# A recorded order that lets the vector engine and GpSimd take turns in their shared SBUF ports, with the decode's additions on the vector engine and row maxima kept in PSUM

## Chip, cores and metric

One core of one Trainium2 chip. The metric is the device time of one execution in microseconds (us). Three executions of the kernel before took 1466.68, 1468.1 and 1468.34 us; the median is 1468.1.

## What is computed

Attention over 4 batches, 12 heads, 448 rows and head size 64, with an RMS norm of q and k; its output, 1792 tokens of 768 values, goes through a feed-forward layer with squared ReLU (d_ff 2048) and then a gated one (d_ff 1536). All in float32.

```python
q_n, k_n = (rmsnorm(q, g_q), rmsnorm(k, g_k))
scores = scale * np.matmul(q_n, k_n.transpose(0, 1, 3, 2))
attn = np.exp(scores - np.max(scores, axis=-1, keepdims=True))
attn = attn / (np.sum(attn, axis=-1, keepdims=True) + 1e-09)
x = np.matmul(attn, v).transpose(0, 2, 1, 3).reshape(B * S, H * D)
r = np.maximum(x @ w_in, 0.0)
x = (r * r) @ w_out
g = x @ w_gate
out = (g * (1.0 / (1.0 + np.exp(-g))) * (x @ w_val)) @ w_out2
```

## The kernel before

A float32 operand is split into a high part (float32r, made by a copy that rounds) and a low part (what is left). A product of the feed-forward layers is then three matmuls of a 128x128 weight block with 448 columns: hi*hi, hi*lo and lo*hi (`mm3`, issued in line 301). Every split needs a subtraction, from SBUF to SBUF.

The weights come as float64 words. `load_weights` decodes them in chunks of 128 rows and 384 columns, two chunks for a tile of 128 d_ff values. A chunk is a transfer to a raw buffer, a scaling (line 252, ScalarE), four vector instructions (lines 262, 265, 268 and 271), an addition (275), a rounding copy (193, ScalarE) and a subtraction (288). The additions and subtractions in 275 and 288 are called the decode's additions below. The key of a weight is `in`, `out` (first layer), `g`, `v`, `o2` (second).

The work has two parts. In the first, attention runs pair of heads by pair of heads: scores of a tile of 128 rows (715, 721), their row maxima (742, vector engine), the maxima times 1/rms (745), the exponentials (751, ScalarE), transposes of the probabilities (811 to 820), their split (851), the products with the values (876 to 886). In its gaps stands the "filler": the first six d_ff tiles of the first layer for batches 0 to 2 (`h_a`, `ya`), and three tiles of batch 3 (`h_lead`, `lead`). Twelve weight tiles are decoded in this part.

The second part sweeps over d_ff tiles, batch after batch: `h` tiles (or `h_g` and `h_v`) accumulate in two PSUM banks, and the vector engine reads them out (338, 354, 364) before the bank can be used again; `y` tiles accumulate over the sweep. 112 chunks are decoded here, each when an older weight's room comes free. That gives three bursts of decoding.

No order is written by hand. A model of the engines in the kernel's Python, run while the kernel is built, decides it: a thread yields an instruction with the engines that may run it and how long that takes, and a free engine takes the ready instruction of the lowest rank. The engine named first is the one the instruction is meant for; another takes it only if the first would be done later than the other by a margin (`spare`: 600 ns for ScalarE, 1500 for the vector engine, 500 for GpSimd). Each engine then executes its instructions in that order.

```python
yield {"G": 956, "V": 469}, lambda e: e.tensor_tensor(out=t, in0=t, in1=a, op=ALU.add)
...
job = min(q, key=lambda job: (job[0].rank, job[2]))
done = free_at[e] = clock[0] + p[0][e]
```

The model before knows nothing that two engines share.

Of the kernel before, what the change touches and what calls it, by code (L numbers as in the profile page):

```python
# [9 lines left out]
F32 = mybir.dt.float32  # L10
# [56 lines left out]
WC = 384  # L67
# [3 lines left out]
def attention_two_ffn_kernel(  # L71
# [51 lines left out]
    engines = {"P": nc.tensor, "A": nc.scalar, "G": nc.gpsimd, "V": nc.vector, "S": nc.sync}  # L123
# [19 lines left out]
    def resume(t, value):  # L143
        while True:
# [11 lines left out]
            elif isinstance(p, tuple):  # L156
                job = [t, p, serial[0], False]
                for e in p[0]:
                    queues[e].append(job)
            else:  # L160
                heapq.heappush(timers, (clock[0] + p, serial[0], t, None))
            return

    def late(job):
        """How long the engine that an instruction is meant for would take to be done with it."""
        costs = job[1][0]
        e = next(iter(costs))
        ahead = [o for o in queues[e] if not o[3] and (o[0].rank, o[2]) < (job[0].rank, job[2]) and next(iter(o[1][0])) == e]
        return max(free_at[e] - clock[0], 0) + sum(o[1][0][e] for o in ahead) + costs[e]

    def dispatch(e):
# [3 lines left out]
        q = [job for job in queues[e] if e == next(iter(job[1][0])) or late(job) > job[1][0][e] + spare[e]]  # L175
# [6 lines left out]
        done = free_at[e] = clock[0] + p[0][e]  # L182
# [18 lines left out]
    def simulate(done):  # L201
        """Issues instructions until done()."""
        while not done():
# [13 lines left out]
            times += [free_at[e] for e in engines if queues[e] and free_at[e] > clock[0]]  # L217
            clock[0] = min(times)
# [1113 lines left out]
```

## Time and profile before

| what | value |
|---|---|
| median of three executions | 1468.1 us |
| span of the profiled execution, first to last instruction | 1462.0 us |
| what the median has around that span | 6.1 us |
| TensorE busy / weight loads | 93% / 79% |
| vector engine / ScalarE / GpSimd busy | 61% / 42% / 45% |
| mean granted TensorE clock | 0.971 |
| last row maximum of the attention starts at | 470.9 us |

The profiled execution's time as a whole is not listed apart from its span; the 6.1 us is the difference to the median. The shares are means over parts with different limits, so the profile is read by stretches. A busy time of the vector engine holds whatever an instruction waits inside itself, after it has started.

### The profile page before, as it was taken

Reading aid. Unit: us, or ns where it says so; the run is one execution under the profiler, and the core shown is the slowest. Engines: PE = TensorE matmul, PEld = TensorE weight load, DVE = VectorE, ACT = ScalarE, POOL = GpSimd, SP = SyncE. Lnnn points to the kernel's source line nnn. Section 1 sums busy time; section 2 is a strip of 40 time slices with the busy share of each in tenths; the row PEclk is TensorE's granted clock in tenths of the full one; section 3 lists DMA queues with packets and bytes.
Section 4 is the critical chain, followed back from the end, with each engine's and each line's share of the span. In section 5 each row is a group of like instructions: output and inputs, shape, how many; then the busy total and the mean of one; then the engine's idle time right before and its main releaser. Section 6 shows DMA issues by size and latency. Waiting matters only on the chain.

```text
span 1462.0 us, 18924 instructions
## 1 busy us (share of the span) xinstructions
PE 1358.5 (93%) x6513; PEld 1148.5 (79%) x6513; DVE 897.2 (61%) x1607; ACT 618.2 (42%) x1376; POOL 656.8 (45%) x580
## 2 busy tenths in 40 slices
PE   8888899999999998889999977899999879999999
PEld 5444667776777887769999866799999768999998
DVE  8999999988887199981011999811117992112121
ACT  5766778777877234333121344312113331111110
POOL 4656674554454177763122666622125762021200
PEclk9999999999999999889999998999999999999999
DMA  6666555534531244343030544502113430122121
GB/s 212 207 188 208 144 164 172 163 117 135 165 116 57 68 119 125 115 123 107 7 108 7 154 127 146 179 16 76 37 39 113 134 110 1 44 71 82 32 76 38
DMA packets 79378, 157.22 MB, mean 108 GB/s; under 512 B 11241, under 2 KB 55090, under 8 KB 79282
## 3 DMA queue, kind: packets, MB, share of 16 engines
q1 hardware_dynamic: 79282, 156.02, 34.9%
q8 instruction: 51, 0.84, 0.2%
q14 instruction: 45, 0.37, 0.1%
HBM read 131.04 MB, written 24.94 MB: 107 GB/s over the span
## 4 chain that ended last, share of the span: by engine, by line
PE 48%; DVE 20%; issue 6%; DMA 1%; POOL 1%; ACT 0%; DVEq 0%; ACTq 0%; POOLq 0%; SPq 0%
PE y L301 15%; PE h_g L301 9%; PE h_v L301 9%; PE h L301 5%; PE ya L301 2%; PE sc L721 1%; PE pt L820 1%; DVE wt_v L262 1%; PE h_a L301 1%; DVE wt_o L265 1%; DVE wt_v L265 1%; DVE wt_out L265 1%; DVE wt_g L262 1%; DVE wt_g L265 1%; DVE wt_o L262 1%
## 5 line engine op out<-in xcount | busy, mean ns | idle before, releaser
L301 PE MATMUL h<-x,hi_in 128*128 128x448 f32 x516 | 159.6, 393 | 31.1 <-DVE r L338 27.8
L301 PE MATMUL h_g<-x,hi_g 128*128 128x448 f32 x576 | 168.8, 375 | 21.1 <-DVE sig L354 19.8
L354 DVE TENSOR_TENSOR sig<-h_g,sig 128x448 f32<-128x448 f32 x48 | 29.9, 622 | 257.0 <-ACT sig L353 257.0
L367 POOL TENSOR_TENSOR s<-sig,s 128x448 fp32r<-128x448 f32 x48 | 57.5, 1198 | 260.4 <-ACT s L193 260.2
L301 PE MATMUL h_v<-x,hi_v 128*128 128x448 f32 x576 | 165.2, 368 | 9.8 <-DVE r L338 6.2
L301 PE MATMUL y<-s,hi_o 128*128 128x448 f32 x576 | 163.6, 365 | 0.0
L301 PE MATMUL y<-s,hi_out 128*128 128x448 f32 x552 | 157.7, 367 | 0.0
L751 ACT ACTIVATE ring<-sc,m,rms 128x448 f32<-128x448 f32 x168 | 121.7, 725 | 64.9 <-DVE m L745 51.4
L301 PEld LDWEIGHTS h<-x,hi_in 128*128 128x128 f32 x516 | 103.6, 203 | 45.8 <-DVE r L338 31.9
L301 PEld LDWEIGHTS h_g<-x,hi_g 128*128 128x128 f32 x576 | 110.4, 193 | 33.8 <-DVE sig L354 23.2
L301 PEld LDWEIGHTS h_v<-x,hi_v 128*128 128x128 f32 x576 | 108.6, 189 | 20.0 <-DVE r L338 6.6
L721 PE MATMUL sc<-kst,qst 128*128 128x448 f32 x368 | 115.3, 407 | 8.7 <-ACT ring L751 8.6
L742 DVE TENSOR_REDUCE m<-sc 128x1 f32<-128x448 f32 x168 | 103.1, 615 | 20.1 <-PE sc L721 17.5
L301 PEld LDWEIGHTS y<-s,hi_o 128*128 128x128 f32 x576 | 108.2, 188 | 8.7
L301 PEld LDWEIGHTS y<-s,hi_out 128*128 128x128 f32 x552 | 104.4, 189 | 8.7
L353 ACT ACTIVATE sig<-h_g 128x448 f32<-128x448 f32 x48 | 26.1, 543 | 195.0 <-PE h_g L301 194.9
L301 PE MATMUL h_g<-x,lo_g 128*128 128x448 f32 x288 | 107.1, 372 | 0.0
L301 PE MATMUL h_v<-x,lo_v 128*128 128x448 f32 x288 | 105.6, 367 | 0.0
L301 PE MATMUL y<-s,lo_o 128*128 128x448 f32 x288 | 105.2, 365 | 0.0
L342 POOL TENSOR_TENSOR s<-r,s 128x448 fp32r<-128x448 f32 x40 | 48.8, 1222 | 122.1 <-DVE r L338 111.5
L301 PE MATMUL h<-x,lo_in 128*128 128x448 f32 x258 | 100.6, 390 | 2.7 <-POOL lo_in L288 2.7
L301 PE MATMUL y<-s,lo_out 128*128 128x448 f32 x276 | 101.1, 366 | 0.0
(177 smaller groups left out, 3134.6 us busy)
## 6 DMA issues: line engine op xcount, KB each, us to landing
kq<-in_kq_t_dram SPq DMA_DIRECT2D x46, 448.0 KB
raw_in<-in_w_in_dram SPq DMA_DIRECT2D x32, 384.0 KB
raw_out<-in_w_out_dram SPq DMA_DIRECT2D x32, 384.0 KB
rkb<-rkd SPq DMA_DIRECT2D x46, 224.0 KB
xr<-x2d SPq DMA_DIRECT2D x42, 224.0 KB
raw_g<-in_w_gate_dram SPq DMA_DIRECT2D x24, 384.0 KB
raw_v<-in_w_val_dram SPq DMA_DIRECT2D x24, 384.0 KB
raw_o<-in_w_out_dram SPq DMA_DIRECT2D x24, 384.0 KB
```

The costliest lines, as they stand in the source:

```text
L262: yield {"V": 269}, lambda e: e.tensor_scalar(out=ti, in0=ai, scalar1=3, scalar2=None, op0=ALU.logical_shift_left)
L265: yield {"V": 469}, lambda e: e.scalar_tensor_tensor(out=ti, in0=ai, scalar=SIGN_BIT, in1=ti, op0=ALU.bitwise_and, op1=ALU.bitwise_or)
L301: return {"P": 187}, lambda e: e.matmul(ps, lhsT=w, rhs=x, start=first, stop=last), 0
L342: yield {"G": 1091, "V": 535}, lambda e: e.tensor_tensor(out=s[:, 1, :], in0=r, in1=as_f32(s[:, 0, :]), op=ALU.subtract)
L353: yield {"A": 424}, lambda e: e.activation(out=t, in_=pg, func=ACTF.Sigmoid)
L354: yield {"V": 535}, lambda e: e.tensor_tensor(out=t, in0=pg, in1=t, op=ALU.mult)
L367: yield {"G": 1091, "V": 535}, lambda e: e.tensor_tensor(out=s[:, 1, :], in0=t, in1=as_f32(s[:, 0, :]), op=ALU.subtract)
L721: e.matmul(sc, lhsT=qs[h][:, c, rows], rhs=ks[h], start=(p + c == 0), stop=(p + 1 == len(parts) and c == 1),)
L742: yield {"V": 531}, lambda e: e.tensor_reduce(out=m[:, 0:1], in_=sc, axis=AX.X, op=ALU.max, negate=True)
L751: yield {"A": 704}, lambda e: e.activation(out=probs(n, 0, S), in_=sc, func=ACTF.Exp, bias=m[:, 1:2], scale=rq, accum_out=sums[g][0][:, i: ...
L820: e.transpose(ps[:, bass.ts(t, 128)], probs((first if j < 3 else second) + t, k, 128), ident)
```

## The change

The model gets a port: while a "ported" instruction runs on GpSimd or the vector engine, neither starts another ported one. Everything on GpSimd is ported; on the vector engine, what is issued under the new letter `W` instead of `V`.

```diff
@@ resume @@
-                    queues[e].append(job)
+                    queues["V" if e == "W" else e].append(job)
@@ new, ahead of late @@
+    port = [0.0]
+    def meant(job):
+        e = next(iter(job[1][0]))
+        return "V" if e == "W" else e
+    def cost(job, e):
+        costs = job[1][0]
+        return costs["W"] if e == "V" and "W" in costs else costs[e]
+    def ported(job, e):
+        return e == "G" or e == "V" and "W" in job[1][0]
@@ dispatch (late in the same way) @@
-        q = [job for job in queues[e] if e == next(iter(job[1][0])) or late(job) > job[1][0][e] + spare[e]]
+        q = [job for job in queues[e] if e == meant(job) or late(job) > cost(job, e) + spare[e]]
+        if port[0] > clock[0]:
+            q = [job for job in q if not ported(job, e)]
...
-        done = free_at[e] = clock[0] + p[0][e]
+        done = free_at[e] = clock[0] + cost(job, e)
+        if ported(job, e):
+            port[0] = done
@@ decode, line 275 (288 in the same way) @@
-            yield {"G": 956, "V": 469}, lambda e: e.tensor_tensor(out=t, in0=t, in1=a, op=ALU.add)
+            yield {"W": 469, "G": 956}, lambda e: e.tensor_tensor(out=t, in0=t, in1=a, op=ALU.add)
@@ mm @@
-        return {"P": 187}, lambda e: e.matmul(ps, lhsT=w, rhs=x, start=first, stop=last), 0
+        return {"P": 203}, lambda e: e.matmul(ps, lhsT=w, rhs=x, start=first, stop=last), 0
@@ all_scores @@
-            sc = tile_at(where, [128, S], F32, f"sc{n}")
+            bank = tile_at(where, [128, 512], F32, f"sc{n}")
+            sc = bank[:, :S]
...
-            spawn(softmax(n, sc, where), n, True)
+            spawn(softmax(n, sc, bank[:, S:S + 1], where), n, True)
@@ softmax @@
-        m = tile_at(m_at, [128, 2], F32, f"m{n}")
-        yield {"V": 531}, lambda e: e.tensor_reduce(out=m[:, 0:1], in_=sc, axis=AX.X, op=ALU.max, negate=True)
+        m = tile_at(m_at, [128, 1], F32, f"m{n}")
+        yield {"V": 531}, lambda e: e.tensor_reduce(out=top, in_=sc, axis=AX.X, op=ALU.max, negate=True)
...
-        yield {"V": 69}, lambda e: e.tensor_tensor(out=m[:, 1:2], in0=m[:, 0:1], in1=rq, op=ALU.mult)
+        yield {"V": 130}, lambda e: e.tensor_tensor(out=m, in0=top, in1=rq, op=ALU.mult)
```

All other SBUF-to-SBUF instructions of the vector engine (decode, scaling of k, splits of k, q, v and x, the rsqrt) go from `V` to `W` with their engines in the order they had. More of the model's durations change: score products 374 to 406 a head (748 to 760 for whole ones), transposes 374 to 480, subtractions on GpSimd 1091 to 1106, rsqrt steps 120 to 97. The vector engine is asked before GpSimd. What is computed stays the same.

How this moves instructions, at three places. Names: `wt_`, `wa_` are a chunk's temporaries, `hi_`, `lo_` the parts of the weight, followed by the key and the d_ff tile (`o22_0` is chunk 0 of tile 2 of `o2`).

The vector engine in the second burst, from the read-out of d_ff tile 11 of the last first-layer sweep on, before:

```order
L338 SCALAR_TENSOR_TENSOR r_1_3_11_8839<-h_1_3_11_8796,r_1_3_11_8839 128x448
L262 TENSOR_SCALAR wt_o22_0_8866<-wa_o22_0_8859 128x384
L265 SCALAR_TENSOR_TENSOR wt_o22_0_8866<-wa_o22_0_8859,wt_o22_0_8866 128x384
L288 TENSOR_TENSOR lo_v2_8846<-wt_v2_1_8816,hi_v2_8845 128x384
L268 TENSOR_SCALAR wa_o22_0_8859<-wt_o22_0_8866 128x384
L262 TENSOR_SCALAR wt_o22_1_8887<-wa_o22_1_8880 128x384
L271 SCALAR_TENSOR_TENSOR wa_o22_0_8859<-raw_o22_0_8817,wa_o22_0_8859 128x384
L265 SCALAR_TENSOR_TENSOR wt_o22_1_8887<-wa_o22_1_8880,wt_o22_1_8887 128x384
```

and the same place in the changed kernel:

```order
L356 SCALAR_TENSOR_TENSOR r_1_3_11_8831<-h_1_3_11_8797,r_1_3_11_8831 128x448
L283 SCALAR_TENSOR_TENSOR wt_v2_0_8839<-wa_v2_0_8828,wt_v2_0_8839 128x384
L306 TENSOR_TENSOR lo_g2_8846<-wt_g2_0_8781,hi_g2_8845 128x384
L286 TENSOR_SCALAR wa_v2_0_8828<-wt_v2_0_8839 128x384
L293 TENSOR_TENSOR wt_g2_1_8790<-wt_g2_1_8790,wa_g2_1_8784 128x384
L289 SCALAR_TENSOR_TENSOR wa_v2_0_8828<-raw_v2_0_8802,wa_v2_0_8828 128x384
L280 TENSOR_SCALAR wt_v2_1_8876<-wa_v2_1_8868 128x384
L293 TENSOR_TENSOR wt_v2_0_8839<-wt_v2_0_8839,wa_v2_0_8828 128x384
L306 TENSOR_TENSOR lo_g2_8846<-wt_g2_1_8790,hi_g2_8845 128x384
```

Lines 293 and 306 (275 and 288 before), which stood almost all on GpSimd, now stand between the decode's other steps.

GpSimd at the start of the first burst, before:

```order
L275 TENSOR_TENSOR wt_in7_1_6356<-wt_in7_1_6356,wa_in7_1_6345 128x384
L342 TENSOR_TENSOR s_1_0_3_6371<-r_1_0_3_6372,s_1_0_3_6371 128x448
L288 TENSOR_TENSOR lo_in7_6363<-wt_in7_1_6356,hi_in7_6362 128x384
L275 TENSOR_TENSOR wt_out7_0_6385<-wt_out7_0_6385,wa_out7_0_6374 128x384
L275 TENSOR_TENSOR wt_out7_1_6403<-wt_out7_1_6403,wa_out7_1_6397 128x384
L288 TENSOR_TENSOR lo_out7_6450<-wt_out7_0_6385,hi_out7_6449 128x384
```

and now:

```order
L1164 TENSOR_TENSOR x_1_0_0_6375<-xr_1_0_0_6344,x_1_0_0_6375 128x448
L360 TENSOR_TENSOR s_1_0_3_6387<-r_1_0_3_6388,s_1_0_3_6387 128x448
L1164 TENSOR_TENSOR x_1_0_4_6601<-xr_1_0_4_6583,x_1_0_4_6601 128x448
L1164 TENSOR_TENSOR x_1_0_5_6774<-xr_1_0_5_6745,x_1_0_5_6774 128x448
L360 TENSOR_TENSOR s_1_0_7_6779<-r_1_0_7_6784,s_1_0_7_6779 128x448
```

What stays on GpSimd are splits of activations.

TensorE behind the last scores of the attention, before:

```order
L721 MATMUL sc167_5920<-kst47_5738,qst1_248 128x448 x2
L301 MATMUL ya2_0_5905<-sa2_0_5244,hi_out0_1400 128x448 x2
L301 MATMUL ya2_0_5905<-sa2_0_5244,lo_out0_1401 128x448
L301 MATMUL ya2_0_5905<-sa2_1_5385,hi_out1_1519 128x448 x2
L301 MATMUL ya2_0_5905<-sa2_1_5385,lo_out1_1520 128x448
```

and now:

```order
L740 MATMUL sc167_5807<-kst47_5639,qst1_248 128x448 x2
L319 MATMUL h_a2_0_5680<-x1_16_4691,hi_in0_514 128x448
L319 MATMUL h_a2_0_5680<-x1_16_4691,lo_in0_515 128x448
L319 MATMUL h_a2_0_5680<-x1_17_4899,hi_in0_514 128x448
L838 MATMUL pt163_5826<-ident_205,ring_245 128x64
```

The filler of batch 2 is at its first `h_a` tile there, not at its first `ya` tile: 95 of its matmuls moved behind the last scores.

## Rows read from the trace of the kernel before

**Rows 1.** By stretch: us; PE, PEld, DVE, ACT, POOL busy (instructions); clock; DMA.
```profile
20.00:220.00 200.00, 172.72 (x743) 108.87 (x743) 197.56 (x412) 144.08 (x356) 128.68 (x111) 0.95 0.60 181
220.00:470.00 250.00, 245.15 (x1276) 186.66 (x1275) 219.20 (x464) 196.97 (x478) 125.19 (x110) 0.99 0.44 135
470.00:510.50 40.50, 40.50 (x205) 35.25 (x206) 10.16 (x20) 14.25 (x31) 9.17 (x9) 1.00 0.19 62
510.50:657.00 146.50, 124.00 (x527) 107.76 (x526) 138.97 (x193) 57.65 (x116) 104.17 (x87) 0.90 0.41 120
657.00:800.00 143.00, 143.00 (x707) 132.54 (x707) 16.82 (x28) 32.24 (x62) 35.20 (x31) 1.00 0.18 59
800.00:950.00 150.00, 124.03 (x571) 111.03 (x570) 143.84 (x205) 58.30 (x114) 99.75 (x85) 0.94 0.49 147
...
1100.00:1215.00 115.00, 98.65 (x458) 88.17 (x457) 101.93 (x144) 43.53 (x87) 74.05 (x64) 0.96 0.38 114
```
**Rows 2.** The longest waits between engines: us in total, times, longest.
```profile
ACT ring L751 <- DVE m L745: 51.4, 64, 2.2
...
PE h L301 <- DVE r L338: 27.8, 11, 4.1
...
ACT wa_v L252 <- DMA raw_v<-in_w_val_dram: 21.2, 15, 2.7
```
**Rows 3.** A stretch of the first burst in order of time: start, us, engine, line, instruction.
```profile
568.41 1.31 POOL L288 TENSOR_TENSOR lo_out<-wt_out,hi_out 128x384 fp32r<-128x384 f32 x1
...
568.90 1.24 DVE L275 TENSOR_TENSOR wt_in<-wt_in,wa_in 128x384 f32<-128x384 f32 x1
...
570.06 0.61 DVE L338 SCALAR_TENSOR_TENSOR r<-h,r 128x448 f32<-128x448 f32 x1
...
570.59 0.62 DVE L262 TENSOR_SCALAR wt_out<-wa_out 128x384 int32<-128x384 int32 x1
...
570.72 0.68 PE L301 MATMUL h<-x,hi_in 128*128 128x448 f32 x2 [1.60 <-DVE r L338]
```
**Rows 4.** Views of the tiles wt_out, r and m: shortest/median/longest ns.
```profile
L265 DVE SCALAR_TENSOR_TENSOR wt_out<-wa_out,wt_out x32: 541/547/1404, 99.3 to 640.6; 128x384 int32<-128x384 int32 x32
...
L275 POOL TENSOR_TENSOR wt_out<-wt_out,wa_out x26: 997/1064/2409, 104.8 to 644.3; 128x384 f32<-128x384 f32 x26
...
L338 DVE SCALAR_TENSOR_TENSOR r<-h,r x43: 603/617/626, 527.7 to 894.7; 128x448 f32<-128x448 f32 x43
...
L745 DVE TENSOR_TENSOR m<-m,rms x168: 137/159/1152, 16.5 to 472.0; 128x1 f32<-128x1 f32 x168
```
**Rows 5.** Groups by line: busy us, mean ns of one, idle before.
```profile
L742 DVE TENSOR_REDUCE m<-sc 128x1 f32<-128x448 f32 x168 | 103.1, 615 | 20.1 <-PE sc L721 17.5 <-PE sc L715 1.5
L745 DVE TENSOR_TENSOR m<-m,rms 128x1 f32<-128x1 f32 x168 | 71.9, 429 | 0.7
L457 DVE TENSOR_REDUCE ss<-nat 128x7 f32<-128x448 f32 x48 | 28.9, 607 | 5.5 <-ACT nat L451 5.5
```
**Rows 6.** The attention in order of time, ScalarE, vector engine and GpSimd.
```profile
101.80 1.27 POOL L646 TENSOR_TENSOR qst<-kq,qst 128x448 fp32r<-128x448 f32 x1
101.97 1.12 DVE L745 TENSOR_TENSOR m<-m,rms 128x1 f32<-128x1 f32 x1
...
103.12 0.72 ACT L751 ACTIVATE ring<-sc,m,rms 128x448 f32<-128x448 f32 x1 [0.60 <-DVE m L745]
...
106.24 0.14 DVE L745 TENSOR_TENSOR m<-m,rms 128x1 f32<-128x1 f32 x1
106.31 0.60 DVE L457 TENSOR_REDUCE ss<-nat 128x7 f32<-128x448 f32 x1
```
**Rows 7.** The first burst in order of time, vector engine.
```profile
562.37 0.35 DVE L262 TENSOR_SCALAR wt_in<-wa_in 128x384 int32<-128x384 int32 x1
...
562.64 0.55 DVE L265 SCALAR_TENSOR_TENSOR wt_out<-wa_out,wt_out 128x384 int32<-128x384 int32 x1
...
563.11 0.55 DVE L265 SCALAR_TENSOR_TENSOR wt_in<-wa_in,wt_in 128x384 int32<-128x384 int32 x1
```

More of the change, by code (lines that the diff above doesn't have):

```diff
@@ L116, in attention_two_ffn_kernel @@
     ctx.enter_context(tc.manual_schedule())
-    engines = {"P": nc.tensor, "A": nc.scalar, "G": nc.gpsimd, "V": nc.vector, "S": nc.sync}
+    engines = {"P": nc.tensor, "A": nc.scalar, "V": nc.vector, "G": nc.gpsimd, "S": nc.sync}
     settle = {"P": 195, "A": 160, "V": 125, "G": 150, "S": 0}
@@ L162, in resume @@
             return
+    port = [0.0]
[7 more added lines that the diff above has]
+        return e == "G" or e == "V" and "W" in job[1][0]
     def late(job):
[L166 to L169, printed above, removed]
+        e = meant(job)
+        ahead = [o for o in queues[e] if not o[3] and (o[0].rank, o[2]) < (job[0].rank, job[2]) and meant(o) == e]
+        return max(free_at[e] - clock[0], 0) + sum(cost(o, e) for o in ahead) + cost(job, e)
     def dispatch(e):
@@ L217, in simulate @@
             times += [free_at[e] for e in engines if queues[e] and free_at[e] > clock[0]]
+            times += [port[0]] * (port[0] > clock[0])
             clock[0] = min(times)
@@ L628, in prep_k @@
         if e == "A":
-            yield {"V": 535, "G": 1091}, lambda e: e.tensor_tensor(out=kr, in0=kr, in1=rk, op=ALU.mult)
+            yield {"W": 535, "G": 1106}, lambda e: e.tensor_tensor(out=kr, in0=kr, in1=rk, op=ALU.mult)
         rk_free.append(rk_at)
@@ L724, in products @@
                         )
-            yield {"P": 748 if full else 374 * len(parts)}, products, 0
+            yield {"P": 760 if full else 406 * len(parts)}, products, 0
             scored[0] = n + 1
@@ L732, in all_scores, with softmax @@
                 kq_free.append(kq_at.pop(g))
-            spawn(softmax(n, sc, where), n, True)
-    def softmax(n, sc, where):
+            spawn(softmax(n, sc, bank[:, S:S + 1], where), n, True)
+    def softmax(n, sc, top, where):
         g, i = divmod(n, PT)
@@ L751, in softmax @@
         yield {"A": 704}, lambda e: e.activation(
-            out=probs(n, 0, S), in_=sc, func=ACTF.Exp, bias=m[:, 1:2], scale=rq, accum_out=sums[g][0][:, i:i + 1]
+            out=probs(n, 0, S), in_=sc, func=ACTF.Exp, bias=m, scale=rq, accum_out=sums[g][0][:, i:i + 1]
         )
@@ L770, in norms @@
         z, at = sums[g]
-        yield {"V": 73}, lambda e: e.tensor_scalar(out=z, in0=z, scalar1=EPS_SUM, scalar2=None, op0=ALU.add)
+        yield {"W": 73}, lambda e: e.tensor_scalar(out=z, in0=z, scalar1=EPS_SUM, scalar2=None, op0=ALU.add)
         yield {"V": 119}, lambda e: e.reciprocal(z, z)
@@ L888, in products @@
                         )
-            yield {"P": 748 if full else 374 * (1 + (j == 3))}, products, 0
+            yield {"P": 760 if full else 406 * (1 + (j == 3))}, products, 0
             pt_free.extend(at)
@@ L940, in outputs @@
         zb, zb_at = zinv.pop(g)
-        yield {"G": 1091, "V": 535}, lambda e: e.tensor_tensor(out=ox, in0=ox, in1=zb, op=ALU.mult)
+        yield {"G": 1106, "W": 535}, lambda e: e.tensor_tensor(out=ox, in0=ox, in1=zb, op=ALU.mult)
         zb_free.append(zb_at)
```

58 lines of the change are left out of this document (29 added, 29 removed).

## Prediction

> **What bounds the kernel now.** I read the busy times by stretch first. Between 657 and 800 us TensorE starts 707 matmuls in 143 us, one per 0.2023 us, at a granted clock of 1.00 [rows 1]: that is its pace when nothing holds it. Three other stretches fall short, and they are the three bursts of decoding: 527 matmuls in 146.5 us (724 at that pace, so 197 or 39.9 us lost), 571 in 150 us (741 would fit, 34.5 us lost), 458 in 115 us (568, 22.3 us lost), with the clock down at 0.90 to 0.96 [rows 1]. In them the vector engine is busy 95%, 96% and 89% of the time, while in the free stretch it is busy 12% [rows 1]. Of the 951 us after the attention, 97 are lost here.
>
> Next the waits: the longest one of TensorE that is worth anything is for the read-out of an `h` bank, 27.8 us in 11 waits [rows 2]. The stretch at 568 us shows why the read-out is late. GpSimd runs a subtraction from 568.41 for 1.31 us; the vector engine starts an addition at 568.90 that ends at 570.14, 0.42 us after GpSimd's end; the read-out `r` follows at 570.06 and the next `h` at 570.72, with TensorE idle for 1.60 us [rows 3]. The tile views say that this is the rule: a decode step on SBUF takes 541 ns at its shortest and 1404 at its longest, a read-out from PSUM 603 to 626 [rows 4]. So the two engines exclude each other for whole instructions where the vector engine works from SBUF to SBUF, and not where it reads PSUM. A busy vector engine here is partly a waiting one.
>
> In the attention the same exclusion hits the softmax. The product of a row maximum with 1/rms is one column; it takes 137 ns at its shortest [rows 4] and 429 on the mean of 168 [rows 5]. At 101.97 us it lasts 1.12 us, beside a GpSimd instruction that runs from 101.80 to 103.07, and ScalarE's exponential starts 0.03 us after its end [rows 6]. ScalarE waits 51.4 us in total for this step [rows 2].
>
> **The change, part by part.** Durations that count on a full engine are spacings from start to start: 0.53 us for 448 columns (570.06 to 570.59 [rows 3]), 0.47 and 0.27 for 384 columns with two inputs or one [rows 7], 0.07 for the product of the maxima [rows 6]. For the other small steps I take 0.10, between that and its shortest duration of 0.14. The sum is against the span, 1462.0 us; the median is 6.1 us above it, and I add these at the end.
>
> *Attention.* From the order I count the vector engine's instructions up to the attention's last output rows. Before: 458 of 448 columns, 58 and 59 of 384 (two inputs, one), 203 small, 168 products: 242.7 + 27.3 + 15.9 + 20.3 + 11.8 = 318 us. Now: 446, 100, 52, 203, 168, the product at 0.14: 236.4 + 47 + 14 + 20.3 + 23.5 = 341 us. The 42 additional decode steps cost 20 us; 22 of 43 scalings of k go to ScalarE, which has room (72% and 79% busy [rows 1]). About 10 us of either sum lie behind the last scores (20 instructions [rows 1]). So of the 470 us up to them, 308 were work and 162 were waits of all kinds, 49 of these in the products of the maxima alone (168 x (429 - 137) ns).
>
> Those 49 us go, because the product now has one input in PSUM, and such instructions were not held [rows 4]. Its price from PSUM is not shown; a reduction of 448 columns takes 615 ns from PSUM and 607 from SBUF [rows 5], 8 ns apart. I take 0.14, its shortest whole duration instead of its spacing. The Trainium skill (Perfetto Trace Analysis, Optimizing Scalar/DVE Operations) gives about 60 ns of access per vector instruction on SBUF and 125 on PSUM. By that rule the product would cost 65 ns more, an estimate of 11 us for 168, where the row's 8 ns make 1.3 us; the 12 us that I have put in cover either.
>
> Of the remaining 113 us of waits I take off 20: GpSimd's instructions up to there fall from 239 to 206, the order is made with the exclusion known, and less filler presses on TensorE. That leaves 93, and the last scores at 332 + 93 = 425 us, where they were at 470. Against that, 95 matmuls of filler moved behind the last scores: 95 x 0.2023 = 19 us more in the stretch that took 40.5 [rows 1]. The attention with its tail ends at 485 instead of 510.5: **-26 us**. Bounds: 60 us of waits give -59; 126 give +7.
>
> *First burst.* GpSimd has 85 instructions from the first to the last split of this sweep, and now 13; the vector engine goes from 192 instructions (75 us at the spacings) to 266 (110 us). If GpSimd's 13 at 1.15 us each (between the median of 1.06 [rows 4] and the 1.31 and 1.27 of the timelines [rows 3, 6]) hold it every time, that makes 15 us more, 125 in all. The last decode step stands just ahead of the read-out of tile 13, and 4 x 18 matmuls remain behind it, 14.6 us, less 2 that overlap: 137.5 against 146.5, **-9 us**. TensorE needs 105.6 for its 522 matmuls and the vector engine 110, so 118 is the lower end. At the upper end the order hurts: 48 decode steps and three splits stand between the read-outs of tiles 3 and 4, 21 us in which TensorE runs dry. I put 155 there.
>
> *Second burst.* TensorE has nine tiles of 36 and six of 54 matmuls, 131 us. The vector engine has 116 us (84 before), GpSimd 23 instructions (90 before), 26 us, of which 34 instructions on PSUM can hide 18. So 124 to 142 us; I take 141, a loss of 10 instead of 34.5: **-24.5 us**, between -34.5 and -12.
>
> *Third burst.* 486 matmuls, 98 us; vector engine 82 us (58 before) and 13 GpSimd instructions (61 before), 15 us. A loss of 6 instead of 22.3: **-16 us**, between -22 and -6.
>
> The other edits (matmuls taken as 203 instead of 187, transposes as 480, shorter rsqrt steps) alter only where the model places things; their effect is in the orders I counted.
>
> Sum: -26 - 9 - 24.5 - 16 = -75.5, a span of 1386.5 and a time of **1392.6 us**. With all ends at once, 1331 to 1472.
>
> **The rivals.**
>
> *The waits only change hands (no gain in the attention).* GpSimd still runs 206 instructions there, some 237 us at 1.15. What the product no longer waits for, the next SBUF step waits for: 119 us of waits leave the end of the attention's tail where it is. Bursts: 0, -17 and -11. Time 1468 - 28 = 1440. For it: a GpSimd as busy as this is met by every second instruction. Against: the steps that then wait are not the ones ScalarE waits for.
>
> *Slower: the waits all stay in the attention.* If all 162 us remain, the last scores come at 494 and the tail ends 43 us late; first burst +9, second -12, third -6. Time 1468 + 34 = 1502. With the bursts like that, it decides from 128 us of waits on. Against it stand the 49 us that belong to one kind of instruction.
>
> *The additions cost in full.* A vector engine busy 139 of 146.5 us [rows 1] has no room, if that time is work: 74 more steps in the first burst, 60 in the second and 48 in the third are 35 + 28 + 22.5 us at 0.47, and 20 + 19 in the attention with its tail. Time 1468 + 125 = 1593. The Trainium skill (Perfetto Trace Analysis, Optimizing Scalar/DVE Operations) says that with a saturated vector engine, giving work to ScalarE or even GpSimd may make sense; by that rule this change goes the wrong way. The trace speaks against it: that busy time holds waits, 75 us being work by the count above. In the same place the Trainium skill adds that the two share a read port, so that moving work between them might not help.
>
> *Hidden anyway: the raw transfers set the bursts' pace.* ScalarE's first decode step waits for a transfer, 21.2 us for `v` alone [rows 2]. If that is the limit, nothing is gained in the bursts nor, with 119 us of waits, in the attention: 1468. Against it: those waits are on ScalarE, which is 39% busy there [rows 1], while the vector engine hardly stands idle.
>
> **How the numbers follow.** Forecast 0.70, waits that change hands 0.17, transfers 0.05, slower 0.06, additions in full 0.02. The range 1350 to 1445 holds most of the forecast's own bounds and the first rival; the rest, some 2 in 10, lies outside. Within 0.2% is about what a measurement of this kernel can tell from no change: faster 0.70 + 0.17 + 0.02, the same 0.03 (the transfers' middle), slower 0.06 + 0.02.
>
> **What would show it.** In the profile of the changed kernel: the product of the maxima at a mean below 200 ns; decode steps near their shortest durations; GpSimd's busy time down by about 225 instructions; 640 matmuls or more in 141 us of the second burst, where 571 took 150; the last row maximum at about 425 us and the end of the filler at about 485. It is wrong if ScalarE still waits some 50 us for the product, if the last maximum stays at 470, or if TensorE still loses 30 us or more in the second burst.

## The result, and the profile after

The changed kernel takes 1419.96 us in the median of four executions (1409.75 to 1429.86), the kernel before 1467.39 beside it: a ratio of 0.9683, 95% interval 0.963 to 0.9736. It is faster, by less than the 75 us that were forecast. The profiled execution took 1429.86 us, the longest of the four; its span is 1427.7, 34.3 us under the 1462.0 of before.

The busy times by stretch of the changed kernel; the stretches are the attention's two halves, its tail (from the last row maximum to the end of the filler), the first burst, the free stretch, and the second and third burst:

```profile
core 0: us, PE busy (x) PEld busy (x) DVE busy (x) ACT busy (x) POOL busy (x), PEclk, DMA share, GB/s
20.00:220.00 200.00, 173.47 (x747) 110.03 (x746) 180.25 (x434) 154.61 (x377) 87.22 (x73) 0.93 0.56 174
220.00:461.90 241.90, 235.25 (x1214) 175.41 (x1212) 199.48 (x482) 199.78 (x485) 125.88 (x110) 0.98 0.47 148
461.90:520.00 58.10, 58.10 (x293) 52.04 (x294) 11.75 (x22) 19.71 (x41) 15.63 (x14) 1.00 0.13 43
520.00:665.00 145.00, 116.73 (x524) 104.17 (x523) 118.97 (x267) 60.04 (x118) 28.59 (x15) 0.89 0.40 121
665.00:800.00 135.00, 135.00 (x655) 122.61 (x654) 14.53 (x24) 28.49 (x54) 34.06 (x30) 1.00 0.20 62
800.00:950.00 150.00, 150.00 (x727) 136.22 (x727) 133.59 (x279) 65.42 (x127) 44.74 (x25) 1.00 0.48 152
1100.00:1215.00 115.00, 115.00 (x558) 104.44 (x557) 83.55 (x173) 41.77 (x82) 31.37 (x15) 1.00 0.33 103
```

Against [rows 1] the second burst starts 727 matmuls in 150 us where it started 571, the third 558 in 115 us where it started 458: TensorE stands still in neither. The first burst still gives 524 in 145 us. The attention did not end earlier: the tail is 58.1 us long, the last row maximum came at 462.0 us (470.9 before), the filler ended at 520.1 (510.7 before). And the free stretch is slower at the same granted clock of 1.00: 135 us for 655 matmuls is 0.2061 us each, where [rows 1] gave 0.2023.

Two lines of the grouping by shape, for the product of the maxima and the exponentials:

```profile
L765 DVE TENSOR_TENSOR m<-sc,rms 128x1 f32<-128x1 f32 x168 | 25.0, 150 | 1.4
L771 ACT ACTIVATE ring<-sc,m,rms 128x448 f32<-128x448 f32 x168 | 121.5, 724 | 32.9 <-DVE m L765 21.7 <-PE pt L834 10.3
```

and the busy times of the page with, under them, four lines of its 40 slices of 35.7 us each:

```profile
PE 1358.5 (95%) x6511; PEld 1142.0 (80%) x6511; DVE 814.3 (57%) x1822; ACT 635.8 (45%) x1408; POOL 437.1 (31%) x355
...
PE   8898798999999995969999999999999999999998
...
DVE  6898899888877249990010399951116992112121
...
POOL 2443454564653320131313142322122240121200
PEclk8999899999999998989999999999999999999999
```

The product has fallen from 429 to 150 ns [rows 5], ScalarE's waits for it from 51.4 to 21.7 us [rows 2]. GpSimd has 355 instructions, 225 fewer than before. In the slices the vector engine's bursts are still there (9 9 9 from the sixteenth on, then two more), but TensorE has a digit under 9 only in the attention, in the first of them and in the last slice, and the clock only in the first two. Of the signs that the prediction listed, those for the mechanism are there; those for the end of the attention (a last row maximum at about 425 us, the end of the filler at about 485) are not.

From the starts of the matmuls in both traces: end of the filler +9.4 us, the 522 matmuls of the first burst -0.9 (145.6 to 144.7), the breaks of the second and third burst -34.6 and -22.3 (to zero), and +15.3 from the slower pace of the 3831 matmuls after the last break (206.7 ns from start to start, 202.7 before). Together -33.1 of the -34.3. Of the +9.4, 3.0 are there before the tenth row maximum (40.4 us after the start, 37.4 before).

### The profile page after: what moved, and what is told of

Its sections match the earlier page's. It is cut to its first block, busy times and chain, and to the rows that moved or that the text cites. A ratio compares the mean times of both kernels' runs of the same rounds, so it can differ in the third digit from the quotient of the medians.

```text
span 1427.7 us, 18828 instructions
## 1 busy us (share of the span) xinstructions
PE 1358.5 (95%) x6511; PEld 1142.0 (80%) x6511; DVE 814.3 (57%) x1822; ACT 635.8 (45%) x1408; POOL 437.1 (31%) x355
## 4 chain that ended last, share of the span: by engine, by line
PE 79%; DVE 10%; DMA 5%; ACT 3%; issue 2%; POOL 1%; SPq 0%; DVEq 0%; ACTq 0%; POOLq 0%
PE y L319 22%; PE h_g L319 13%; PE h_v L319 13%; PE h L319 9%; PE ya L319 4%; PE sc L740 4%; PE pt L840 4%; PE h_a L319 3%; PE o L901 2%; PE o L906 2%; PE pt L838 1%; DVE wa_out L289 1%; DMA nat<-in_q_n_dram 1%; DVE sc L762 1%; ACT ring L771 1%
## 5 line engine op out<-in xcount | busy, mean ns | idle before, releaser
L319 PE MATMUL h<-x,hi_in 128*128 128x448 f32 x516 | 153.3, 379 | 23.2 <-DVE r L356 23.1
L385 POOL TENSOR_TENSOR s<-sig,s 128x448 fp32r<-128x448 f32 x47 | 73.3, 1560 | 327.5 <-ACT s L210 327.4
L319 PE MATMUL h_g<-x,hi_g 128*128 128x448 f32 x576 | 165.5, 368 | 0.0
L771 ACT ACTIVATE ring<-sc,m,rms 128x448 f32<-128x448 f32 x168 | 121.5, 724 | 32.9 <-DVE m L765 21.7
L319 PEld LDWEIGHTS h<-x,hi_in 128*128 128x128 f32 x516 | 100.2, 195 | 34.6 <-DVE r L356 24.7
L360 POOL TENSOR_TENSOR s<-r,s 128x448 fp32r<-128x448 f32 x38 | 60.6, 1598 | 209.8 <-DVE r L356 203.3
L762 DVE TENSOR_REDUCE sc<-sc 128x1 f32<-128x448 f32 x168 | 104.2, 625 | 33.0 <-PE sc L740 26.9
L1164 POOL TENSOR_TENSOR x<-xr,x 128x448 fp32r<-128x448 f32 x52 | 69.0, 1332 | 157.2 <-ACT x L210 157.2
L319 PEld LDWEIGHTS y<-s,hi_o 128*128 128x128 f32 x576 | 108.1, 188 | 10.9
L319 PEld LDWEIGHTS h_g<-x,hi_g 128*128 128x128 f32 x576 | 108.1, 188 | 10.9
L319 PEld LDWEIGHTS h_v<-x,hi_v 128*128 128x128 f32 x576 | 108.1, 188 | 10.9
L356 DVE SCALAR_TENSOR_TENSOR r<-h,r 128x448 f32<-128x448 f32 x43 | 26.5, 621 | 139.8 <-ACT s L355 139.7
```

The costliest lines, as they stand in the source:

```text
L319: return {"P": 203}, lambda e: e.matmul(ps, lhsT=w, rhs=x, start=first, stop=last), 0
L356: yield {"V": 535}, lambda e: e.scalar_tensor_tensor(out=r, in0=ps, scalar=0.0, in1=r, op0=ALU.max, op1=ALU.mult)
L360: yield {"G": 1106, "W": 535}, lambda e: e.tensor_tensor(out=s[:, 1, :], in0=r, in1=as_f32(s[:, 0, :]), op=ALU.subtract)
L385: yield {"G": 1106, "W": 535}, lambda e: e.tensor_tensor(out=s[:, 1, :], in0=t, in1=as_f32(s[:, 0, :]), op=ALU.subtract)
L762: yield {"V": 531}, lambda e: e.tensor_reduce(out=top, in_=sc, axis=AX.X, op=ALU.max, negate=True)
L771: yield {"A": 704}, lambda e: e.activation(out=probs(n, 0, S), in_=sc, func=ACTF.Exp, bias=m, scale=rq, accum_out=sums[g][0][:, i:i + 1])
```

## The experiments

A table first, so that the runs can be read side by side. "Filler end" is the end of the attention's tail; "first burst" the time of the 522 matmuls after it; "breaks" what TensorE lost in the second and third burst, as the sum of start-to-start distances beyond their normal length; "pace" the distance in the free stretch. All four are of the one profiled execution, whose pace can differ from that of the others; over the 3831 matmuls the two paces are 15 us apart, so the medians of two kernels tell less about an edit than the columns behind them.

| kernel | median us (range) | ratio to before, 95% | filler end | first burst | breaks | pace ns |
|---|---|---|---|---|---|---|
| before | 1467.39 (1464.18 to 1468.34) | | 510.7 | 145.6 | 34.6 + 22.3 | 202.7 |
| changed | 1419.96 (1409.75 to 1429.86) | 0.963 to 0.9736 | 520.1 | 144.7 | 0 + 0 | 206.7 |
| `again` | 1413.48 (1408.01 to 1427.55) | 0.9601 to 0.9712 | 518.5 | 143.9 | 0 + 0 | 206.7 |
| `b_vfirst` | 1418.39 (1409.34 to 1423.65) | 0.9654 to 0.9721 | 513.8 | 133.6 | 7.4 + 0.3 | 206.7 |
| `no_port` | 1431.1 (1427.11 to 1435.68) | 0.9735 to 0.9792 | 519.4 | 138.8 | 15.9 + 7.2 | 206.7 |
| `b_psum` | 1455.63 (1450.52 to 1462.29) | 0.9909 to 0.9962 | 503.7 | 146.2 | 34.0 + 22.5 | 202.7 |
| `m_sbuf` | 1427.49 (1415.58 to 1433.81) | 0.9698 to 0.9768 | 520.0 | 142.9 | 2.4 + 0 | 202.7 |
| `ahead2` | 1395.88 (1395.05 to 1407.9) | 0.9485 to 0.9572 | 510.5 | 129.7 | 5.1 + 0 | 202.7 |
| `old_pe` | 1411.9 (1404.56 to 1415.26) | 0.9612 to 0.9649 | 506.5 | 142.4 | 5.5 + 0 | 202.7 |
| `split` | 1398.5 (1396.33 to 1408.89) | 0.9498 to 0.9573 | 503.4 | 143.7 | 1.7 + 0 | 202.7 |
| `combo` | 1384.94 (1373.63 to 1394.2) | 0.934 to 0.9479 | 501.0 | 128.4 | 0 + 0 | 206.7 |
| `combo_a2` | 1383.27 (1382.29 to 1398.63) | 0.9395 to 0.9501 | 501.9 | 131.3 | 0 + 0 | 202.7 |
| `combo_np` | 1413.27 (1410.29 to 1420.93) | 0.9574 to 0.9673 | 505.1 | 136.5 | 17.2 + 5.4 | 202.7 |

### Which part frees the bursts

`b_vfirst`, the kernel before with one edit, in both places:

```diff
-            yield {"G": 956, "V": 469}, lambda e: e.tensor_tensor(out=t, in0=t, in1=a, op=ALU.add)
+            yield {"V": 469, "G": 956}, lambda e: e.tensor_tensor(out=t, in0=t, in1=a, op=ALU.add)
```

> The kernel before with the decode's additions meant for the vector engine first, and nothing else: no port, maxima in SBUF, the old durations. Theory (additions alone): GpSimd has 210 instructions fewer, the second and third burst lose under 15 us together instead of 57, and the time is 1412 to 1425. Rival (the port does it): the bursts lose 30 us or more and the time is 1440 or more. In the attention both expect no gain, the last row maximum at 470 us or later.

Measured: 1418.39 us, 7.7 us of breaks in the second and third burst where there were 56.9, and 133.6 us for the first. So the additions alone, in an order that knows nothing of turns, give about what the whole change gives. The decode steps on the vector engine last 540 and 565 ns on the mean in the first two bursts, and 771 and 784 in the kernel before. The attention got no gain, as both readings expected: the last row maximum came at 477.9 us, 7 us later than before.

`no_port`, the changed kernel with

```diff
-        return e == "G" or e == "V" and "W" in job[1][0]
+        return False
```

> The changed kernel with a port that never blocks: the order model again knows nothing that two engines share; the additions stay on the vector engine first, the maxima in PSUM, the new durations in the model. GpSimd gets 15 instructions more. Theory (the bursts gain because the additions leave GpSimd): 1415 to 1425, second and third burst still without a loss. Rival (they gain because the two engines take turns): the decode steps on SBUF are held again and 20 to 40 us of the gain are gone, 1440 to 1460.

Measured: 1431.1 us, 23.1 us of breaks. Neither reading holds in full: most of the gain stays, and yet the turns are worth something that I had not expected.

`combo_np` against `combo` (below) tells it from one and the same attention; the edit is the one of `no_port`.

> The kernel with the attention of before and maxima in PSUM, additions on the vector engine from its end on, but with a port that never blocks there either; against its twin with the port it tells what the turns alone bring, from the same attention. GpSimd's instructions are as many, only their places differ. Theory (the turns are worth 10 to 25 us in the second and third burst once the additions are gone from GpSimd, as in the changed kernel without the port, where these two lost 23): the filler ends at 500 to 504 us, the second and third burst lose 15 to 25 us, 1395 to 1412. Rival (the additions alone carry the bursts, and what the changed kernel without the port lost came from elsewhere): under 8 us lost, 1374 to 1396.

Measured: 1413.27 against 1384.94 us. The busy times of the stretches with the two later bursts, `combo_np`:

```profile
780.00:955.00 175.00, 164.48 (x780) 149.25 (x779) 135.72 (x274) 65.38 (x128) 61.32 (x34) 0.97 0.42 130
1040.00:1215.00 175.00, 171.81 (x837) 157.79 (x836) 102.63 (x208) 53.21 (x105) 47.20 (x27) 0.99 0.24 75
```

what TensorE waits for in it from 800 to 960 us:

```profile
PE h_g L320 <- DVE sig L373: 4.6, 4, 2.6
PE h_v L320 <- DVE r L357: 4.5, 1, 4.5
PE h L320 <- DVE r L357: 1.4, 1, 1.4
```

and the busy times of `combo`, which has no such wait there:

```profile
780.00:955.00 175.00, 175.00 (x848) 158.95 (x848) 132.44 (x270) 70.41 (x138) 48.25 (x37) 1.00 0.46 146
1040.00:1215.00 175.00, 175.00 (x848) 158.95 (x848) 102.36 (x208) 55.38 (x108) 33.65 (x24) 1.00 0.29 92
```

With the same vector engine (274 and 270 instructions) TensorE starts 780 matmuls in the one and 848, without a break, in the other, although the latter's pace is the slower one. What it waits for is the read-outs, as before the change [rows 2, 3]. The breaks come to 22.6 us, and the first burst, whose order differs too, takes 8.1 us more. Once the additions are gone from GpSimd, the turns are worth about 23 us in the two later bursts of an order made with the new durations. In `b_vfirst`, which has the old durations, 7.7 us of breaks were left for them; why the new durations without turns do worse was not followed up.

### What the row maxima in PSUM bring

`b_psum`, the kernel before with the maxima in the score's bank, the model's 69 ns for the product left alone:

```diff
-        yield {"V": 531}, lambda e: e.tensor_reduce(out=m[:, 0:1], in_=sc, axis=AX.X, op=ALU.max, negate=True)
+        yield {"V": 531}, lambda e: e.tensor_reduce(out=top, in_=sc, axis=AX.X, op=ALU.max, negate=True)
...
-        yield {"V": 69}, lambda e: e.tensor_tensor(out=m[:, 1:2], in0=m[:, 0:1], in1=rq, op=ALU.mult)
+        yield {"V": 69}, lambda e: e.tensor_tensor(out=m, in0=top, in1=rq, op=ALU.mult)
```

> The kernel before with the row maxima in PSUM and the product reading them there, and nothing else; the order of every engine is that of the kernel before. Prediction's reading (49 us of waits in the product are on the path): last row maximum at 425 to 445 us and 1435 to 1450. Theory now (TensorE with its filler is the bound from 220 us on, and a wait gone there is filled by the next): the product falls from 429 to about 150 ns, ScalarE's waits for it by 30 us or more, and the last row maximum moves by under 10 us, 1458 to 1468.

Measured: 1455.63 us, a ratio of 0.9935 (0.9909 to 0.9962), last row maximum at 463.9 us and the filler's end at 503.7, 7 us earlier than before. The time is a little under the theory's range, the last row maximum within it. The product in its tile's view:

```profile
L746 DVE TENSOR_TENSOR m<-sc,rms x168: 139/146/159, 20.9 to 465.0; 128x1 f32<-128x1 f32 x168
```

and ScalarE's waits for it:

```profile
ACT ring L752 <- DVE m L746: 34.9, 34, 4.7
```

No product lasts longer than 159 ns, where the longest took 1152 [rows 4]: 47 us of busy time are gone (168 x (429 - 147) ns). 7 us of these reach the end of the attention, or 10 when both executions are counted from their tenth row maximum (40.8 us here, 37.4 before, with the same order of every engine); the medians are 10 us apart (1465.4 for the kernel before in the same set of runs). ScalarE's waits fell only from 51.4 to 34.9 us, since a product also starts late.

`m_sbuf` takes the same edit back in the changed kernel, its order left as it is.

> The changed kernel with the row maxima and their product back in SBUF, the order of all engines as in the change. Theory (the lock that the product no longer meets is worth the same 7 to 10 us as in the kernel before): product at a mean of 300 to 380 ns instead of 150, the filler's end at 524 to 530 us, 1416 to 1438 by the pace. Rival (with the port the model keeps GpSimd out of the product's way by itself, or other waits take its place): the end at 516 to 521 us, 1408 to 1430.

```profile
L765 DVE TENSOR_TENSOR m<-m,rms 128x1 f32<-128x1 f32 x168 | 63.7, 381 | 1.4
```

The product is back at 381 ns and the filler ends at 520.0 us, as in the changed kernel: by that number alone the rival holds. But this execution had a lead from its beginning. GpSimd's first wait for a transfer was as short as in `ahead2`, an execution of the same order, and shorter than in the changed kernel's first one and in `again` (19.5). First the changed kernel, then `m_sbuf`, both from 0 to 40 us:

```profile
POOL nat L470 <- DMA nat<-in_q_n_dram: 19.8, 1, 19.8
POOL nat L470 <- DMA nat<-in_q_n_dram: 14.1, 1, 14.1
```

The tenth row maximum starts at 35.8 us in `m_sbuf` and at 40.4, 40.8 and 37.0 in the three executions with the maxima in PSUM. From there to the filler's end `m_sbuf` takes 484.2 us and they take 479.7, 477.7 and 473.5. So with the maxima in SBUF this part is 4 to 11 us longer, which speaks for the theory; the median, too, is 7.5 to 14 us above the two of the changed kernel. It is one execution against three, and the intervals of the times overlap, so the worth of the maxima in PSUM is shown there no closer than some 4 to 11 us.

### Why the attention did not end earlier

The changed kernel's and `split`'s row for 100 to 260 us, in which most of the twelve weight tiles of the attention are decoded. First the changed kernel:

```profile
100.00:260.00 160.00, 137.38 (x612) 93.84 (x611) 144.90 (x330) 123.69 (x296) 75.56 (x64) 0.90 0.52 158
260.00:460.00 200.00, 198.82 (x1037) 149.42 (x1037) 161.08 (x389) 166.79 (x407) 106.15 (x94) 0.99 0.46 145
```

then `split`, the changed kernel with one edit:

```diff
-            yield {"W": 469, "G": 956}, lambda e: e.tensor_tensor(out=t, in0=t, in1=a, op=ALU.add)
+            yield {"W": 469, "G": 956} if bursts else {"G": 956, "W": 469}, lambda e: e.tensor_tensor(out=t, in0=t, in1=a, op=ALU.add)
...
     att.close()
+    bursts.append(0)
```

```profile
100.00:260.00 160.00, 146.94 (x685) 101.95 (x684) 147.82 (x344) 131.59 (x318) 89.75 (x77) 0.96 0.55 169
260.00:460.00 200.00, 198.11 (x1037) 149.70 (x1036) 151.59 (x367) 158.97 (x385) 102.47 (x90) 1.00 0.45 132
```

> The changed kernel with the decode's additions on GpSimd first while the attention runs and on the vector engine first only from its end on; port, new durations and maxima in PSUM as in the change. Of the 48 additions of the twelve weight tiles decoded in the attention GpSimd then has 34 instead of 1; filler ahead of the last scores 464 instead of 445. The tiles 42 to 84 took 132 to 133 us in the changed kernel, 130 to 133 in three others with the additions on the vector engine, 115 to 117 in three with them on GpSimd, and in the former the clock was longer at 0.50. Theory (the additions on the vector engine hold up this part): 115 to 122 us for the tiles 42 to 84, the filler's end 8 to 15 us before the changed kernel's 518 to 520; first burst still in clumps, 1395 to 1415 by the pace of TensorE. Rival (the port or the new durations of TensorE hold it up): 127 us or more, 1408 to 1428.

Measured: 1398.5 us; the tiles 42 to 84 took 123.3 us, a little above the range; the filler's end came at 503.4 us, 15 to 17 before the changed kernel's 518.5 and 520.1. In the 160 us TensorE starts 612 matmuls with the additions on the vector engine and 685 with them on GpSimd; the granted clock is 0.90 and 0.96 on the mean of its two levels, 1.2 and 2.4 GHz, so the lower one was granted for longer in the changed kernel, in stretches where TensorE was busy 137 of 160 us. From 260 us on both start 1037 in 200 us, with TensorE at 99%: there it is the bound, and the waits of others cost nothing. So the additions that free the bursts hold the attention up while its weights are decoded. `b_vfirst` says the same without port and new durations: there the one edit takes the tiles 42 to 84 from 121.8 us, in the kernel before, to 133.1. Through which wait is not settled. The changed kernel has six waits of ScalarE for a decode step of the vector engine there, up to 3.4 us, with the exponentials behind them on ScalarE (its waits from 100 to 260 us):

```profile
ACT p L210 <- PE pt L840: 7.6, 10, 1.3
ACT hi_out L210 <- DVE wt_out L293: 7.0, 6, 3.4
ACT ring L771 <- DVE m L765: 5.0, 5, 1.8
```

In `split` that wait is not among the larger ones; no run took it away by itself. How far one order's filler end scatters shows in `ahead2`, whose attention is ordered as in the changed kernel and ended at 510.5 us: 8 to 10 us earlier than in three other executions of that order (`again`, `m_sbuf` and the first). Part of this is the beginning: the hundredth matmul after the first starts at 25.8 and 26.9 us in the first and `again`, at 21.1 in `ahead2`. The 503.4 lie under all four values of that order (510.5 to 520.1), but the size of the effect is 7 to 17 us by the filler's end, and 8 to 14 when counted from the tenth row maximum (465.4 us in `split`, which has it at 38.0), no closer.

`old_pe`, the changed kernel with the old durations of TensorE:

```diff
-        return {"P": 203}, lambda e: e.matmul(ps, lhsT=w, rhs=x, start=first, stop=last), 0
+        return {"P": 187}, lambda e: e.matmul(ps, lhsT=w, rhs=x, start=first, stop=last), 0
...
-            yield {"P": 480 + 96 * (j == 3) + 54 * bool(rider)}, turn, 0
+            yield {"P": 374 + 96 * (j == 3) + 54 * bool(rider)}, turn, 0
```

(and 374 and 748 for the products of a head.)

> The changed kernel with the old durations of TensorE in the model (187 a matmul, 374 a head's scores, 374 a transpose); 538 filler matmuls stand ahead of the last scores instead of 445, the port and the additions as in the change. Theory (the filler that the new durations move behind the last scores costs in the tail what it frees before): the last row maximum 10 to 20 us later, the filler's end within 6 us of the changed kernel's 518 to 520. Rival (the moved filler is what made the attention late): the filler's end at 505 or earlier. In the first burst 63 decode steps stand ahead of the read-out of tile 4, so it should lose some us more; 1410 to 1430.

Measured: 1411.9 us, last row maximum at 466.8, filler's end at 506.5, so 4 to 14 us before that of the changed kernel's order, and not within 6 us of its 518 to 520. Of the tail the theory was right (39.7 us instead of 58.1): the filler that is moved behind the last scores costs 18 us there. In return the last row maximum comes 5 to 14 us earlier with it moved (452.5 to 462.0 in the four executions of the changed order), so that by the filler's end the move costs more than it frees. How much more is open: this execution, too, had an early beginning (tenth row maximum at 34.2 us), and from there to the filler's end it takes 472.3 us, only 1 to 7 less than the three of the changed kernel.

It also limits what `split` shows. The tiles 42 to 84 took 124.0 us here, with the additions on the vector engine, and 123.3 in `split`; in its row TensorE starts 655 matmuls, between the 612 and the 685:

```profile
100.00:260.00 160.00, 139.48 (x655) 97.97 (x654) 134.41 (x328) 125.30 (x300) 83.34 (x72) 0.94 0.53 162
```

So either edit alone shortens this part by 7 to 9 us against the 131 to 133 of the changed kernel's order. The 124.0 are a value that the expectation of `split` does not name. The additions are thus one thing that holds this part up, shown by two edits, and not the only one: the order as a whole counts, and what the new durations of TensorE do to it no run separates.

### The first burst

Waits of TensorE of the changed kernel from 510 to 650 us, then those of the vector engine from 461 on:

```profile
PE h L319 <- DVE r L356: 23.1, 3, 10.2
```

```profile
DVE r L356 <- ACT s L355: 32.9, 5, 23.8
```

The vector engine stands 23.8 us behind a read-out whose square is not there yet, while the tail of the filler runs (it is busy 11.75 of the 58.1 us), and starts to decode at 522 us; then TensorE waits up to 10.2 us for read-outs that stand behind up to 48 decode steps.

`ahead2` breaks these clumps up:

```diff
-W_AHEAD = 6
+W_AHEAD = 2
```

> The changed kernel with one number altered: a weight's decoding is ranked 2 steps ahead of its use instead of 6. From the order, the attention and the second and third burst stay as they are; in the first burst the vector engine's work between two read-outs of h is 6 to 8 us for tiles 4 to 9 where it was 0.5 to 21.5 (48 decode steps ahead of the read-out of tile 4), and TensorE's work for a tile is 7.4 us. Theory (the first burst lost its gain because decode steps stand in clumps ahead of the read-outs): the first 522 matmuls behind the attention take 118 to 130 us instead of 145, 1390 to 1402. Rival (the raw transfers or the vector engine's sum of work set the burst): 140 us or more, 1408 to 1422, with ScalarE waiting longer for the transfers.

Measured: 129.7 us for the 522 matmuls instead of 144.7, 1395.88 us. The clumps were the cause for 15 us. What stays looks like the vector engine's sum of work: its row for 510 to 640 us has it busy for 122.22 of 130 us, and TensorE hardly waits for read-outs any more (0.8 us) but for ScalarE's rounded weights (its longest wait from 510 to 650 us, under the row), as ScalarE waits for the vector engine's additions (18.2 and 10.9 us). No run shortened that work by itself.

```profile
510.00:640.00 130.00, 114.33 (x524) 99.78 (x523) 122.22 (x265) 59.73 (x117) 33.14 (x17) 0.96 0.45 135
PE h L319 <- ACT hi_in L210: 11.6, 6, 3.7
```

ScalarE waited 31.8 us for raw transfers there (15 waits for `out`, 15 for `in`), more than the 27.0 of the changed kernel, and the burst was faster all the same: the transfers do not set its pace.

### A version below both

`combo` orders the attention as before (old durations, GpSimd first, no port), with the maxima in PSUM, and takes the change from the attention's end on:

```diff
-        return e == "G" or e == "V" and "W" in job[1][0]
+        return bool(bursts) and (e == "G" or e == "V" and "W" in job[1][0])
...
-        return {"P": 203}, lambda e: e.matmul(ps, lhsT=w, rhs=x, start=first, stop=last), 0
+        return {"P": 203 if bursts else 187}, lambda e: e.matmul(ps, lhsT=w, rhs=x, start=first, stop=last), 0
```

with the additions as in `split` and the attention's other durations as before.

> The attention ordered as in the kernel before (old durations, no port, the decode's additions on GpSimd first) with the maxima in PSUM; the port, the new durations and the additions on the vector engine from the end of the attention on. Theory (the change made the attention no faster because it also loads the vector engine and moves filler behind; alone the PSUM maxima gain): the end of the filler at 501 to 506 us as with the PSUM maxima alone, where the changed kernel has 518 to 520; second and third burst without loss; 1395 to 1410. Rival (the port's turns are what the bursts need from the attention's side too, or the order of the attention matters little): the filler ends at 512 us or later, 1410 or more.

Measured: 1384.94 us (1373.63 to 1394.2), under the expected range; the filler's end at 501.0, and a first burst of 128.4 us, which the expectation did not hold: its read-outs of tiles 4 to 8 came to stand behind 8 to 21 decode steps instead of up to 48 (later ones behind up to 36). Its row for the first burst, to set beside that of `ahead2`:

```profile
500.00:630.00 130.00, 118.28 (x531) 104.74 (x530) 120.60 (x260) 60.23 (x118) 33.37 (x23) 0.93 0.45 135
```

`combo_a2` adds `W_AHEAD = 2`.

> The kernel with the attention of before, maxima in PSUM and the port and additions from its end on, and decoding ranked 2 steps ahead instead of 6. Theory: the two gains add, filler ending at 501 to 506 us and a first burst of 118 to 130 us: 1375 to 1392, below both kernels. Rival (decoding that is ranked later only moves the loss to later tiles, where 24 to 29 steps now stand ahead of a read-out): the first burst at 140 us or more, 1395 to 1410.

Measured: 1383.27 us, not to be told from `combo` (the intervals overlap); its first burst is no shorter, 131.3 us. Both medians are 29 to 37 us below the two of the changed kernel, and `combo_a2` ran at the faster pace in its profile, `combo` at the slower one. Four executions with this attention and the maxima in PSUM ended the filler at 501.0 to 505.1 us, against 510.7 in the one of before.

### The same kernel again

> The changed kernel once more, nothing altered. In its profile the matmuls of the free stretches start 206.7 ns apart, in that of the kernel before 202.7, both at a granted clock of 1.00; over the 4194 matmuls behind the attention the 4 ns make 17 us. Theory (the pace belongs to the execution): its times spread again over 1409 to 1430, and a profiled execution near 1410 shows a spacing near 203. Rival (the pace belongs to the kernel): 206.7 ns in this profile too, and a spread that comes from elsewhere.

Measured: 1427.55 us in the profiled execution, 1408.01, 1415.46 and 1411.51 in the others, and a pace of 206.7 ns again. This run alone does not decide between theory and rival. The others do. `no_port` has both paces in one execution, each in a free stretch at a granted clock of 1.00:

```profile
665.00:800.00 135.00, 135.00 (x655) 122.63 (x654) 14.52 (x24) 27.10 (x51) 34.76 (x31) 1.00 0.20 62
970.00:1100.00 130.00, 130.00 (x643) 120.47 (x642) 22.20 (x41) 27.00 (x53) 29.52 (x24) 1.00 0.15 48
```

135 us for 655 is 0.2061 each, 130 for 643 is 0.2022. And `ahead2` and `split`, with the same matmuls, ran at the lower figure. So the pace belongs neither to the kernel nor to an execution, but to a stretch of it.

## Why the prediction was right and wrong

Right in sign and class, and 27 us too low: 1392.6 forecast, 1419.96 measured, within the range of 1350 to 1445. That it lies in the range is in part luck: the attention missed by 35 us and lies beyond its own bound of +7, and the later two bursts gave 16 us more than forecast, as much as their own bounds allow.

*Attention, -26 forecast, +9.4 measured.* The step that failed is "those 49 us go". They went as busy time of the vector engine (47 us, in `b_psum`), but only 7 to 10 of them were on the path: from 260 us on at the latest TensorE is the bound with its filler, and I had taken every wait of the vector engine up to 470 us as delay of the last scores. That TensorE was busy 245.15 of the 250 us from 220 us on stood in [rows 1] already. The second failing step is the cost of the 42 additional decode steps. I took them as 20 us of work in a sum and gave as much back with "of the remaining 113 us of waits I take off 20"; `split` shows that moving them back is worth 7 to 17 us at the end, though `old_pe` shortens the tiles 42 to 84 as much with the additions left where they are. The 19 us of filler behind the last scores were right (the tail grew from 39.8 to 58.1), and `old_pe` shows that its absence does not free as much earlier on.

*First burst, -9 forecast, -0.9 measured.* What I had put at the upper end, the 48 decode steps ahead of the read-out of tile 4, was the likely case, and not an extreme: `ahead2` gains 15 us by removing the clumps alone.

*Second burst, -24.5 forecast, -34.6 measured; third, -16 and -22.3.* The mechanism was right, its size was not. The losses of 10 and 6 us that I left for GpSimd's remaining instructions did not come: without the turns 17.2 and 5.4 us are lost (`combo_np`), with them nothing (`combo`).

*The pace.* 15.3 us of the profiled execution lie in a term that the prediction doesn't have, since it took 0.2023 us for a matmul as fixed.

*Two terms of the sum.* The 6.1 us around the span were too many: the profiled execution of the changed kernel took 1429.86 us with a span of 1427.7, so 2.2 us stand around it. With as much around its 1462.0, the profiled execution of before took 1464.2, and the rest of the 6.1 was its distance from the median; the forecast is 4 us too high by this. And the outer range "1331 to 1472" is 6 to 7 us too high at either end: the bounds of the four parts add up to 1324 and 1466.

*The rivals.* "The waits only change hands" was right about the attention and the first burst, and wrong about the later two; the time lies between it (1440) and the forecast. "The additions cost in full" is refuted by `b_vfirst`: the vector engine takes over the additions of three bursts, and is busy for 861.7 us in all there, where it was busy 897.2. The Trainium skill (Perfetto Trace Analysis, Optimizing Scalar/DVE Operations) says that with a saturated vector engine giving work to ScalarE or even GpSimd may make sense, and adds the shared port as a caution. In these bursts the caution decides: the mean decode step in the second burst took 784 ns before and 537 after. "The raw transfers set the pace" fell with `ahead2`. That the product would be dearer from PSUM did not show: in the kernel before it lasted 148 ns on the mean of the 80 times that it started while no GpSimd instruction ran, from PSUM 147 to 151.

## What to carry to other kernels

Where two engines exclude each other, look first at which work can leave the one that holds the other up longest (an addition here took 1064 ns on GpSimd [rows 4] and some 550 on the vector engine); turns in the order come second, and they pay for what is left. A wait that is removed is worth what it costs at the place where its stage ends last, so ask for every stretch which engine is at 99% before summing waits over the whole. An edit that frees one phase can hold up another, so let it hold only in the phase that needs it, as `combo` does.

## What was not expected of the hardware

In the kernel before, the exclusion can be read off by whether an instruction of the vector engine starts while one of GpSimd runs. A decode step of line 262 lasted 1011 ns on the mean of the 66 times that it did and 348 on the mean of the 70 that it did not (at most 360); the product of the maxima 683 (88 times) and 148 (80). A read-out from PSUM (line 338) shows no difference: 610 and 618. Nor does a reduction of 448 columns from SBUF (line 457: 605 and 608), so "from SBUF to SBUF", as the prediction has it, is too wide.

TensorE has two paces for one and the same sequence of matmuls at a granted clock of 1.00: 202.7 ns from start to start (a mixture of 199, 203 and 207) and 206.7 (nearly all the same). In the profiled executions here, nearly every stretch without a break of more than some 280 ns holds one of the two from end to end, up to 3831 matmuls; where it changes, there is a break. A kernel with bursts of breaks mixes both, and one whose breaks are gone keeps for the rest of its time the pace with which it left the last: over 3831 matmuls the two are 15.3 us apart. That fits the spread of some 20 us in the times of the changed kernel and of `combo` (1373.63 and 1376.34, 1393.54 and 1394.2), while the kernel before, with three bursts of breaks, stays within 4 us in its first four executions and within 5 to 10 in the later sets. That the other executions of a kernel differ by their pace is not shown, since only one of each was profiled. What sets the pace at a break was not tried.
